# An S5 layer beside a SwiGLU: which DMA ring carries the first loads, and in which order the first products run

## The chip, the cores and the metric

The kernel runs on one core of one Trainium2 chip. The metric is the time of one execution on the device in microseconds (us), the median over runs. A profile is one further execution, taken by the hardware profiler, with its own time.

A core has five engines with their own instruction queues: TensorE (PE, matrix products; its weight loads are listed as PEld), VectorE (DVE), ScalarE (ACT), GpSimd (POOL) and SyncE (SP). Transfers between device memory and on-chip memory (DMAs) are issued here from two queues, SP's and ScalarE's. In the profile, q1 is the ring of transfers that SP issued, q10 the ring of those that ScalarE issued; both are worked off by the same sixteen transfer engines.

## What is computed

With x of shape (1, 2048, 512) in bfloat16, cut to what matters:

```python
xn = layernorm(x)                                   # over the 512 columns, no scale, eps 1e-5
# A: a diagonal state space layer with P = 512 complex states
dt = exp(log_dt); Lam = Lambda_re + 1j * Lambda_im
Lam_bar = exp(dt * Lam); B_bar = ((Lam_bar - 1) / Lam)[:, None] * (B_re + 1j * B_im)
Bu = xn @ B_bar.T
h[t] = Lam_bar * h[t - 1] + Bu[t]                   # over 2048 rows
yA = 2 * real(h @ C.T) + xn * Dskip
# B: a SwiGLU with F = 1792
yB = (silu(xn @ w1) * (xn @ w3)) @ w2
out = x + yA + yB
```

w1 and w3 are 512x1792, w2 is 1792x512.

## The kernel before

The 2048 rows are handled in four blocks of 512 (`x_blk[0..3]`), each block as four chunks of 128 rows. The columns D = 512 are four contraction tiles of 128 (`NDT = 4`, with the halves `lo` = tiles 0 and 1 and `hi` = tiles 2 and 3, `H = 2`). The hidden width F is fourteen tiles f of 128.

For each block: statistics and normalisation on DVE (`stats`, `aggr`, `normed`) with the reciprocal root on ScalarE for block 0 (`rstd_act`), a transpose into `xnT`, the gate and up products `g_ps` and `u_ps` on TensorE (`glu_mm`, L372) and their activations on ScalarE (`glu_up`), the state space input products `bu_ps` (L411), rotation and scan on DVE, and last the output products `y_ps` (L488, L493), the residual sum (L498) and the store (L499). The order of the work is written out by hand (`manual_schedule`): each engine runs its instructions in the order in which the program issues them, and small DVE tasks are taken from a queue by given costs.

The change lies in the first ten microseconds, the way to the first products of block 0:

- *Loads.* `load_rows` (L77) brings chunks of block 0: chunks 0 and 1 singly and chunks 2 and 3 together (256 KB). `load_w13` (L95) brings columns of w1 and w3; for the first four f tiles in two pieces each, by contraction half (`w1` low, `w1` high, `w3` low, `w3` high, 256 KB each, 1 KB per partition and contraction tile). `load_prm` (L109) brings one of three parameter vectors (`A_Lambda_re`, `A_Lambda_im`, `A_log_dt`, 1 KB each) into rows of `prm`, which TensorE later transposes (L544).
- *Queues.* SP issues rows 0, rows 1, w1 low, w1 high, w3 low, w3 high, then the next four f tiles of w1 and w3, block 1's rows, and so on. ScalarE issues Lambda_re, rows 2 and 3 together, Lambda_im, log_dt. Eight completion semaphores are used in turn for the DMAs, so that a DMA's issue waits for the landing of the one that had its semaphore before. The first column pieces of tiles 4 to 7 (w1) wait in this way for w1 low, w3 high for rows 1, log_dt for rows 0.
- *Transposes.* `turn` (L251) turns a chunk on TensorE into PSUM and `put` (L256 on ScalarE, L258 on DVE) copies it to `xnT`. Chunks 0 and 1 are turned and copied in halves; chunk 1's halves go through the two PSUM buffers of f = 2 (`t1`, views of `begun[2]`), so the products of f = 2 can't start before chunk 1 has been copied out.
- *First products.* `ahead` runs the products of f = 0, 1, 2 (`B3`) over the chunks that are there. `keep_warm` (L150) runs products of constants ahead of them, whose result isn't used.

Before, TensorE ran both halves of chunk 0's and chunk 1's transposes first, then, for f = 0, 1, 2, all low halves (chunk 0, then chunk 1, each 128 columns), then the high halves over both chunks at once (256 columns), then w3:

```python
    ahead((w1_sb,), B3, 0, 1, lo)
    ahead((w1_sb,), B3, 1, 1, lo, True)
    ahead((w1_sb,), B3, 0, 2, hi)
```

The last argument (`joins`) keeps a product from opening its accumulation anew, since chunk 0's sums in the same buffer are still open.

Of the kernel before, what the change touches and what calls it, by code (L numbers as in the profile page):

```python
# [20 lines left out]
def kernel(  # L21
# [24 lines left out]
    nc = tc.nc  # L46
# [6 lines left out]
    CPB = TBLK // P  # L53
    NSB = TBLK // SB
    NDT = D // P
# [20 lines left out]
    def load_rows(c0, c1, eng):  # L76
        eng.dma_start(out=x_blk[0][:, c0:c1, :], in_=xv[:, 0, c0:c1, :])  # L77
# [4 lines left out]
    w1_sb = const.tile([P, NDT, F], BF16, name="w1_sb")  # L82
    w3_sb = const.tile([P, NDT, F], BF16, name="w3_sb")
    w2_sb = const.tile([P, NFT, D], BF16, name="w2_sb")
    w1v = B_w1.rearrange("(t p) f -> p t f", p=P)
    w3v = B_w3.rearrange("(t p) f -> p t f", p=P)

    H = NDT // 2

    def load_w13(f0, f1, parts=1):  # L90
        fs = slice(f0 * P, f1 * P)
        for w_sb, wv in ((w1_sb, w1v), (w3_sb, w3v)):
            for i in range(parts):
                ds = slice(i * NDT // parts, (i + 1) * NDT // parts)
                nc.sync.dma_start(out=w_sb[:, ds, fs], in_=wv[:, ds, fs])  # L95

    dskip_row = const.tile([P, D], BF16, name="dskip_row")
    bt = [const.tile([P, NDT, PS], BF16, name=f"bt{ri}") for ri in range(2)]
# [9 lines left out]
    def load_prm(i, src, eng):  # L108
        eng.dma_start(out=prm[i * NPT:(i + 1) * NPT, :], in_=src.rearrange("(t p) -> t p", p=P))  # L109

    load_prm(0, A_Lambda_re, nc.scalar)
    load_rows(2, CPB, nc.scalar)
    load_prm(1, A_Lambda_im, nc.scalar)
    load_prm(2, A_log_dt, nc.scalar)
    load_w13(0, 4, 2)
    load_w13(4, 8)
    nc.sync.dma_start(out=x_blk[1], in_=xv[:, 1, :, :])
    load_w13(8, NFT)
    nc.sync.dma_start(out=dskip_row, in_=A_Dskip.partition_broadcast(P))
    load_turned(bt[0], A_B_re)  # L120
# [26 lines left out]
    def keep_warm(n, width=512):  # L147
        one = nc.const_aps.tensor_like(1.0, like=ident[:, 0:1])
        for _ in range(n):
            nc.tensor.matmul(out=begun[0][0][:, :width], lhsT=one.to_broadcast([P, P]), rhs=one.to_broadcast([P, width]),  # L150
                             start=True, stop=True)
# [10 lines left out]
    def stats(c):  # L162
        sums[c] = work.tile([P, 6], FP32, name="stats", bufs=4)
        nc.vector.bn_stats(out=sums[c], in_=x_blk[c // CPB][:, c % CPB, :])  # L164
# [4 lines left out]
    def rstd_act(c0, c1):  # L169
        y = rstd_all[:, c0:c1]  # L170
        nc.scalar.activation(out=y, in_=mv_all[:, c0:c1, 1], func=ACT.Ln, bias=LN_EPS)
        nc.scalar.activation(out=y, in_=y, func=ACT.Exp, scale=-0.5)
# [15 lines left out]
    def normed(c, parts=1):  # L188
        xn = work.tile([P, D], BF16, name="xn", bufs=8)
        for i in range(parts):  # L190
            ds = slice(i * D // parts, (i + 1) * D // parts)
            nc.vector.tensor_scalar(out=xn[:, ds], in0=x_blk[c // CPB][:, c % CPB, ds], scalar1=mv_all[:, c, 0:1],
                                    scalar2=rstd_all[:, c:c + 1], op0=ALU.subtract, op1=ALU.mult)
        return xn
# [54 lines left out]
    def turn(c, pxt, d0=0, d1=NDT):  # L249
        for dt in range(d0, d1):  # L250
            nc.tensor.transpose(out=pxt[:, dt - d0, :], in_=xn0[c][:, dt * P:(dt + 1) * P], identity=ident)  # L251

    def put(c, pxt, eng, d0=0, d1=NDT):
        dst = xnTs[0][:, d0:d1, c * P:(c + 1) * P]
        if eng is nc.scalar:
            nc.scalar.activation(out=dst, in_=pxt, func=ACT.Copy)  # L256
        else:
            nc.vector.tensor_copy(out=dst, in_=pxt)  # L258
# [110 lines left out]
    def glu_mm(b, f, w_sb, ps, ts, dts=range(NDT), joins=False):  # L369

        for dt in dts:
            nc.tensor.matmul(out=ps[:, ts], lhsT=w_sb[:, dt, f * P:(f + 1) * P], rhs=xnTs[b][:, dt, ts],  # L372
                             start=(dt == 0 and not joins), stop=(dt == NDT - 1))
# [128 lines left out]
    def ahead(w_sbs, fs, c, n=1, dts=range(NDT), joins=False):  # L502
        for f in fs:
            for w_sb in w_sbs:
                glu_mm(0, f, w_sb, begun[f][w_sb is w3_sb], slice(c * P, (c + n) * P), dts, joins)
# [13 lines left out]
    xn0[1] = normed(1, 2)  # L519
    turn(0, tb, H, NDT)  # L520
    put(0, tb, nc.scalar, H, NDT)
    keep_warm(2, P)
    turn(1, t1[0], 0, H)
    put(1, t1[0], nc.scalar, 0, H)
    turn(1, t1[1], H, NDT)
    put(1, t1[1], nc.scalar, H, NDT)
    stats(2)
    aggr(2)
    rstd_act(2, 3)
    stats(3)  # L530
    B3 = (0, 1, 2)
    lo, hi = range(H), range(H, NDT)
    ahead((w1_sb,), B3, 0, 1, lo)
    ahead((w1_sb,), B3, 1, 1, lo, True)
    ahead((w1_sb,), B3, 0, 2, hi)
    xn0[2] = normed(2)
    aggr(3)
    rstd_act(3, 4)
    ahead((w3_sb,), B3, 0, 2, lo)
    turn(2, t2)  # L540
    put(2, t2, nc.vector)
    xn0[3] = normed(3)
    ahead((w3_sb,), B3, 0, 2, hi)
    nc.tensor.transpose(out=pprm, in_=prm, identity=ident)  # L544
# [63 lines left out]
```

## Time and profile before

| | |
|---|---|
| median of 3 runs | 211.63 us (211.57 to 211.89) |
| the profiled execution's own time | 212.11 us |
| its span, first to last instruction | 210.3 us |
| PE busy | 206.6 us (98%), 1036 instructions |
| DVE busy | 173.5 us (82%) |
| ACT busy | 93.4 us (44%) |
| granted TensorE clock | 1.000 |
| moved by DMA | 13.69 MB, mean 65 GB/s |

A line of a group or of the timeline names the source line, the engine, the operation, out<-in by the program's names (w1, w3 and w2 are all `w_sb`), and the form. Matmuls are pipelined: the duration of one reaches from its start to its result, and the spacing of starts tells the rate. Queue lines (SPq, ACTq) are the issue of a DMA and not its transfer. An idle time in square brackets names what ended it.

### The profile page before, as it was taken

Reading aid. Unit: us, or ns where it says so; the run is one execution under the profiler, and the core shown is the slowest. Engines: PE = TensorE matmul, PEld = TensorE weight load, DVE = VectorE, ACT = ScalarE, POOL = GpSimd, SP = SyncE. Lnnn points to the kernel's source line nnn. Section 1 sums busy time; section 2 is a strip of 40 time slices with the busy share of each in tenths; the row PEclk is TensorE's granted clock in tenths of the full one; section 3 lists DMA queues with packets and bytes.
Section 4 is the critical chain, followed back from the end, with each engine's and each line's share of the span. In section 5 each row is a group of like instructions: output and inputs, shape, how many; then the busy total and the mean of one; then the engine's idle time right before and its main releaser. Section 6 shows DMA issues by size and latency. Waiting matters only on the chain.

```text
span 210.3 us, 2878 instructions
## 1 busy us (share of the span) xinstructions
PE 206.6 (98%) x1036; PEld 97.7 (46%) x1036; DVE 173.5 (82%) x346; ACT 93.4 (44%) x167; POOL 6.0 (3%) x27
## 2 busy tenths in 40 slices
PE   8999999999999999999999999999999999999994
PEld 3864444444444444444444444444444444444453
DVE  4699989989999999999999999999999999121111
ACT  3599967666666200066666600036666620000000
POOL 2010320000000000000000000000000000000000
PEclk9999999999999999999999999999999999999999
DMA  5999599944000000000004200100000000000110
GB/s 165 294 366 219 109 178 325 217 106 100 0 3 0 0 25 25 28 26 0 0 0 77 28 1 24 50 25 5 0 0 0 0 3 25 27 25 25 34 44 25
DMA packets 25014, 13.69 MB, mean 65 GB/s; under 512 B 15912, under 2 KB 25000, under 8 KB 25000
## 3 DMA queue, kind: packets, MB, share of 16 engines
q1 hardware_dynamic: 24704, 13.24, 26.1%
q10 hardware_dynamic: 296, 0.27, 0.4%
q8 instruction: 8, 0.13, 0.3%
q14 instruction: 6, 0.05, 0.1%
HBM read 7.74 MB, written 2.10 MB: 47 GB/s over the span
## 4 chain that ended last, share of the span: by engine, by line
PE 96%; DMA 2%; SPq 0%; DVE 0%; issue 0%
PE g_ps L372 23%; PE u_ps L372 23%; PE y_ps L488 23%; PE y_ps L493 13%; PE bu_ps L411 13%; DMA w_sb<-in_B_w_dram 2%; SPq L77 0%; PE xt_ps L251 0%; DVE o L498 0%; PE xt_ps L544 0%
## 5 line engine op out<-in xcount | busy, mean ns | idle before, releaser
L372 PEld LDWEIGHTS <-w_sb 128*128 128x128 bf16 x502 | 46.4, 98 | 50.6 <-DMA w_sb<-in_B_w_dram 0.6
L372 PE MATMUL g_ps<-xnT,w_sb 128*128 128x512 bf16 (+2 forms) x254 | 58.2, 354 | 0.3 <-DMA w_sb<-in_B_w_dram 0.3
L372 PE MATMUL u_ps<-xnT,w_sb 128*128 128x512 bf16 (+2 forms) x248 | 58.4, 358 | 0.0
L488 PE MATMUL y_ps<-w_sb,hgT 128*128 128x512 bf16 (+2 forms) x238 | 51.2, 366 | 0.0
L390 ACT ACTIVATE up<-u_ps 128x512 bf16<-128x512 f32 x56 | 34.0, 607 | 14.9 <-PE u_ps L372 14.9
L413 ACT ACTIVATE u<-bu_ps 128x512 bf16<-128x512 f32 x32 | 19.1, 597 | 46.3 <-PE bu_ps L411 46.3
L388 ACT ACTIVATE sl<-g_ps 128x512 bf16<-128x512 f32 x56 | 34.0, 608 | 9.9 <-PE g_ps L372 9.2
L445 DVE TENSOR_TENSOR_SCAN ab<-r_col,h,ab 128x256 bf16<-128x256 f32 x56 | 37.7, 733 | 0.2
L488 PEld LDWEIGHTS <-hgT 128*128 128x128 bf16 x238 | 22.8, 98 | 25.9
L498 DVE TENSOR_TENSOR o<-y_ps,x_blk 128x512 bf16<-128x512 f32 (+2 forms) x17 | 11.1, 654 | 24.3 <-PE y_ps L493 24.3
L493 PE MATMUL y_ps<-ct,h 128*128 128x512 bf16 (+2 forms) x136 | 30.4, 366 | 0.0
L411 PE MATMUL bu_ps<-xnT,bt 128*128 128x512 bf16 x128 | 28.1, 379 | 0.0
L397 DVE TENSOR_TENSOR hgT<-sl,up 128x512 bf16<-128x512 bf16 x56 | 22.9, 414 | 2.1 <-ACT up L390 2.1
L493 PEld LDWEIGHTS <-h 128*128 128x128 bf16 x136 | 13.0, 98 | 14.7
L411 PEld LDWEIGHTS <-bt 128*128 128x128 bf16 x128 | 12.5, 98 | 15.1
L164 DVE BATCH_NORM_STATS2 stats<-x_blk 128x6 f32<-128x512 bf16 x16 | 10.6, 675 | 2.5 <-DMA x_blk<-in_A_x_dram 2.5
L454 DVE TENSOR_TENSOR ab<-ab,tab_s 128x2048 bf16<-128x2048 bf16 x8 | 9.8, 1222 | 0.2
L450 DVE TENSOR_TENSOR ab<-ab,tab_c 128x2048 bf16<-128x2048 bf16 x8 | 9.8, 1222 | 0.1
L427 DVE TENSOR_TENSOR ab<-u,tab_x 128x2048 bf16<-128x2048 bf16 x8 | 9.7, 1219 | 0.0
L430 DVE TENSOR_TENSOR ab<-u,tab_y 128x2048 bf16<-128x2048 bf16 x8 | 9.7, 1218 | 0.0
L201 DVE TENSOR_TENSOR x_blk<-xd,x_blk 128x512 bf16<-128x512 bf16 x16 | 6.8, 426 | 0.5
L200 DVE TENSOR_TENSOR xd<-xn,dskip_row 128x512 bf16<-128x512 bf16 x16 | 6.7, 418 | 0.0
(76 smaller groups left out, 81.3 us busy)
## 6 DMA issues: line engine op xcount, KB each, us to landing
out_dram<-o SPq DMA_DIRECT2D x15, 128.0 KB, 1.7
w_sb<-in_B_w_dram SPq DMA_DIRECT2D x1, 1792.0 KB, 9.3
x_blk<-in_A_x_dram SPq DMA_DIRECT2D x3, 512.0 KB, 6.3
w_sb<-in_B_w_dram SPq DMA_DIRECT2D x2, 768.0 KB, 7.8
w_sb<-in_B_w_dram SPq DMA_DIRECT2D x4, 256.0 KB, 5.0
w_sb<-in_B_w_dram SPq DMA_DIRECT2D x2, 512.0 KB, 4.1
x_blk<-in_A_x_dram SPq DMA_DIRECT2D x2, 128.0 KB, 2.2
x_blk<-in_A_x_dram ACTq DMA_DIRECT2D x1, 256.0 KB, 4.7
```

The lines of the kernel that those rows point to most:

```text
L164: nc.vector.bn_stats(out=sums[c], in_=x_blk[c // CPB][:, c % CPB, :])
L372: nc.tensor.matmul(out=ps[:, ts], lhsT=w_sb[:, dt, f * P:(f + 1) * P], rhs=xnTs[b][:, dt, ts], start=(dt == 0 and not joins), stop=(dt == ...
L388: nc.scalar.activation(out=sl16, in_=g_ps, func=ACT.Silu)
L390: nc.scalar.activation(out=up16, in_=u_ps, func=ACT.Copy)
L397: nc.vector.tensor_tensor(out=hg[b][:, f, :], in0=sl16, in1=up16, op=ALU.mult)
L411: nc.tensor.matmul(out=u_ps, lhsT=bt[ri][:, dt, pt * P:(pt + 1) * P], rhs=xnTs[b][:, dt, :], start=(dt == 0), stop=(dt == NDT - 1))
L413: nc.scalar.activation(out=u16[:, :, pt, ri, :], in_=u_ps.rearrange("p (s t) -> p s t", s=NSB), func=ACT.Copy)
L445: nc.vector.tensor_tensor_scan(out=a[:, pt, 2 * ri + 1, :], data0=r_b, data1=a[:, pt, 2 * ri, :], initial=init, op0=ALU.mult, op1=ALU.add)
L450: nc.vector.tensor_tensor(out=a[:, :, 0::2, :], in0=a[:, :, 1::2, :], in1=tab_b("c"), op=ALU.mult)
L488: nc.tensor.matmul(out=y_ps[:, ds], lhsT=hg[b][:, f, cl * P:(cl + 1) * P], rhs=w2_sb[:, f, ds], start=(f == 0), stop=False)
L493: nc.tensor.matmul(out=y_ps[:, ds], lhsT=h_tiles[i][:, pt, ri, h_ts], rhs=ct[ri][:, pt, ds], start=False, stop=(pt == NPT - 1 and ri == 1))
L498: nc.vector.tensor_tensor(out=o16[:, ds], in0=y_ps[:, ds], in1=x_blk[b][:, cl, ds], op=ALU.add)
```

## The change

Rows 2 and 3, Lambda_im and log_dt move from ScalarE's queue to SP's, and w1 low and w1 high from SP's to ScalarE's. ScalarE issues Lambda_re, w1 low, w1 high. SP issues rows 0, rows 1, rows 2 and 3, Lambda_im, log_dt, w3 low, w3 high, and from there on the same as before. With the other order the semaphores fall differently: the w1 piece of tiles 4 to 7 waits for the landing of rows 2 and 3, w3 low for that of rows 0.

On TensorE the first products of w1 run in another order: chunk 0's low half for f = 0 and 1 stands between the two halves of chunk 1's transposes; then, for f = 0 and 1, chunk 0 high, chunk 1 low, chunk 1 high; then f = 2 over both chunks and all four contraction tiles. The work from w3's products on is in the same order as before.

```diff
-    def load_w13(f0, f1, parts=1):
+    def load_w(w_sb, wv, f0, f1, eng, ds=slice(0, NDT)):
         fs = slice(f0 * P, f1 * P)
-        for w_sb, wv in ((w1_sb, w1v), (w3_sb, w3v)):
-            for i in range(parts):
-                ds = slice(i * NDT // parts, (i + 1) * NDT // parts)
-                nc.sync.dma_start(out=w_sb[:, ds, fs], in_=wv[:, ds, fs])
+        eng.dma_start(out=w_sb[:, ds, fs], in_=wv[:, ds, fs])
+
+    def load_w13(f0, f1):
+        load_w(w1_sb, w1v, f0, f1, nc.sync)
+        load_w(w3_sb, w3v, f0, f1, nc.sync)
...
+    low, high = slice(0, H), slice(H, NDT)
     load_prm(0, A_Lambda_re, nc.scalar)
-    load_rows(2, CPB, nc.scalar)
-    load_prm(1, A_Lambda_im, nc.scalar)
-    load_prm(2, A_log_dt, nc.scalar)
-    load_w13(0, 4, 2)
+    load_w(w1_sb, w1v, 0, 4, nc.scalar, low)
+    load_w(w1_sb, w1v, 0, 4, nc.scalar, high)
+    load_rows(2, CPB, nc.sync)
+    load_prm(1, A_Lambda_im, nc.sync)
+    load_prm(2, A_log_dt, nc.sync)
+    load_w(w3_sb, w3v, 0, 4, nc.sync, low)
+    load_w(w3_sb, w3v, 0, 4, nc.sync, high)
     load_w13(4, 8)
...
     put(0, tb, nc.scalar, H, NDT)
+    B3 = (0, 1, 2)
+    lo, hi = range(H), range(H, NDT)
     keep_warm(2, P)
     turn(1, t1[0], 0, H)
     put(1, t1[0], nc.scalar, 0, H)
+    ahead((w1_sb,), (0, 1), 0, 1, lo)
     turn(1, t1[1], H, NDT)
     put(1, t1[1], nc.scalar, H, NDT)
     stats(2)
     aggr(2)
     rstd_act(2, 3)
     stats(3)
-    B3 = (0, 1, 2)
-    lo, hi = range(H), range(H, NDT)
-    ahead((w1_sb,), B3, 0, 1, lo)
-    ahead((w1_sb,), B3, 1, 1, lo, True)
-    ahead((w1_sb,), B3, 0, 2, hi)
+    ahead((w1_sb,), (0, 1), 0, 1, hi)
+    ahead((w1_sb,), (0, 1), 1, 1, lo)
+    ahead((w1_sb,), (0, 1), 1, 1, hi)
+    ahead((w1_sb,), (2,), 0, 2)
```

## Prediction, made before the changed kernel was run

> **What bounds the kernel now.** I read the page first: its chain of waits says which engine sets the end.
>
> ```profile
> PE 96%; DMA 2%; SPq 0%; DVE 0%; issue 0%
> PE g_ps L372 23%; PE u_ps L372 23%; PE y_ps L488 23%; PE y_ps L493 13%; PE bu_ps L411 13%; DMA w_sb<-in_B_w_dram 2%; SPq L77 0%; PE xt_ps L251 0%; DVE o L498 0%; PE xt_ps L544 0%
> ```
>
> TensorE carries 96%, and ahead of it stands one load, of w1 or w3 (2%, 4.8 us). The timeline of PE where that load ends is next (start, duration, line, operation, count, idle before it):
>
> ```profile
> 5.54 0.42 PE L251 MATMUL g_ps<-ident,xn 128*128 128x128 bf16 x2
> 5.76 0.41 PE L251 MATMUL u_ps<-ident,xn 128*128 128x128 bf16 x2
> 6.48 1.51 PE L372 MATMUL g_ps<-xnT,w_sb 128*128 128x128 bf16 x18 [0.31 <-DMA w_sb<-in_B_w_dram]
> 7.83 0.83 PE L372 MATMUL u_ps<-xnT,w_sb 128*128 128x256 bf16 x6
> ```
>
> The reader is to see one wait of 0.31 us ahead of the first product at 6.48, and none behind it. The busy time in windows, asked from there to PE's last instruction, shows how long that lasts (stretch, its length, then busy time by engine):
>
> ```profile
> 6.48:207.66 201.18, 201.18 (x1013) 95.21 (x1013) 170.11 (x334) 90.19 (x159) 4.64 (x19) 1.00 0.26 61
> ```
>
> PE is busy for all of 201.18 us. So any delay of the first products reaches the end one to one (no later idle time absorbs it), and nothing that the change does later than these products can help. The tail behind 207.66 (DVE, last store) stays.
>
> Third, the loads that feed the first products. Issues, from the timeline of all engines:
>
> ```profile
> 0.72 0.87 SPq L77 DMA_DIRECT2D x_blk<-in_A_x_dram  x2
> 0.94 0.55 ACTq L109 DMA_DIRECT2D prm<-in_A_Lambda_re_dram  x1
> 1.53 0.44 ACTq L77 DMA_DIRECT2D x_blk<-in_A_x_dram  x1
> 1.64 5.73 SPq L95 DMA_DIRECT2D w_sb<-in_B_w_dram  x6
> ```
>
> SP's six are w1 low half (1.64), w1 high (2.11), w3 low (2.62), w3 high (3.40), then the next 512 columns of each (6.45, 6.86). By the trace's semaphore events rows 2–3 land at 6.24, w1 low at 6.43, w1 high 7.11, w3 low 7.78, w3 high 8.44. The first products use them at 6.48, 7.16, 7.83 and 8.72: each of the first three lands about 0.05 us ahead of its user. The last fact needed is how the two rings share the transfer engines. The DMA queues of the window 4.0 to 4.5 us, when rows 2–3 (q10, ScalarE's ring) and w1 low (q1, SP's) both move (packets, MB, share of 16 engines):
>
> ```profile
> q10 hardware_dynamic: 85, 0.09, 48.4%
> q1 hardware_dynamic: 80, 0.08, 47.7%
> ```
>
> An even split. And on one ring alone a 256 KB piece takes 0.67 us (6.43, 7.11, 7.78, 8.44).
>
> **The change part by part.**
>
> *Which ring.* Rows 2–3 and w1 low change places. They are the same size (256 KB in pieces of 1 KB), issued within 0.11 us of each other, so I let them swap landings: w1 low at 6.24, 0.19 us earlier. The bounds are 5.47, where fifteen of its sixteen completion counts for rows 2–3 stood before (one transfer engine runs 0.76 us behind the rest in all five pieces), and 6.43 (no gain).
>
> *w1 high* is issued on ScalarE at about 2.0 instead of 2.11, which is worth nothing, because data and not issue is late. Before, it followed w1 low on a ring that was alone by then, and w3 low waited behind it. Now w3 low heads the other ring (issued at about 2.9: behind rows 2–3, two parameter loads of 0.27 to 0.55 us each on the issuing queue, and the landing of rows 0, whose semaphore it reuses, at 2.87), so the two share. On the late engine: at 6.24 w1 low is done, and rows 2–3 have the 0.19 us left that separated the two before. Shared, that takes 0.38: rows 2–3 land at 6.62, and w1 high has 0.19 of its 0.67 us. The other 0.48 is shared with w3 low: 0.96. w1 high lands at 6.62 + 0.96 = 7.58 instead of 7.11; w3 low still at 7.78, since the sum of bytes is unchanged. The bounds are 6.91 (ScalarE's ring served alone from 6.24 on) and 7.78 (as late as w3 low). I take 7.58, since the even split is what the rows show.
>
> The Trainium skill speaks against expecting more from a second ring (DMA: Bandwidth & Descriptors, "Issuing engines are not separate DMA queues"): DMAs from any engine end up on the same sixteen transfer engines and interleave, and several issuers save issue time only. The even split above agrees, and the sum by that rule is the same.
>
> *Order of the first products.* On PE the first 24 units (one unit is 128 columns, 0.056 us apart in the trace; 256 columns take 0.109) stay 24: before 12x128 and 6x256, now 16x128 and 4x256. Two more instructions cost nothing, because spacing goes by columns. What moves is what can run while w1 high is missing. Before: all twelve low products, 0.67 us, which covered the 6.48 to 7.16 gap between the pieces. Now: four (f = 0 and 1, rows 0), 0.22 us, and the two transposes of row block 1's high half, which stood in the idle time at 5.76 and now stand behind the wait on w1 low, 0.11 us. Everything else on PE queues behind the first high product. Row by row: restart 6.24 + 0.05 = 6.29; four products to 6.51; two transposes to 6.62; wait for w1 high to 7.58 + 0.05 = 7.63; then 12x0.056 + 4x0.109 = 1.11, to 8.74. Before, w3's first product started at 7.83. So **+0.91 us**.
>
> *Who waits behind the moved transposes.* ScalarE's copy of that half (L256) moves from 6.28 to about 6.9, ends at 7.3, and its next user on PE runs at about 8.1; ScalarE's rstd for row 2 follows at about 7.4. Free here; without the wait for w1 high it would cost (third rival).
>
> *Rows 2–3 later* (6.62 instead of 6.24): DVE's statistics (L164) start at 6.64 instead of 6.27, the normalised row 2 ends at 8.46 instead of 8.09. PE transposes it at 8.49 + 0.91 = 9.40. Free, with 0.9 us to spare. *Parameters on SP* (lam_im and log_dt): read by the transpose at 9.27 (L544), landing near 7. Free by over 2 us. *The next w1 piece* (columns 512 to 1023) waited for w1 low's landing and now waits for rows 2–3's: issue 6.64 instead of 6.45, landing 10.57 + 0.19, first use 12.33 + 0.91. Free; w3's behind it likewise. w3 low is needed at 8.74, w3 high at 9.63; both have landed.
>
> **Sum.** +0.91 us on the profiled execution: span 210.3 to 211.2, own time 212.11 to 213.02. The median of the runs is 211.63, 0.48 below that execution; on it, **212.5 us**.
>
> **The rivals.**
>
> 1. *Rings alternate in whole shares.* If a transfer engine drains w1 high's sixteen pieces before it turns to w3 low, w1 high lands at 7.11 as before, PE restarts at 7.16 and reaches w3 at 8.27: +0.44, 212.07. Against: from 5.13 to 5.73 us the late engine's last eight data packets on q10 start 85 ns apart, by the trace's packet records, and a packet takes 46 ns, so single packets alternate. The Trainium skill gives the rule in the same page ("Queues, rings and completion order"): an engine round-robins between rows and takes some 9 to 17 descriptors from one before it switches. The 85 ns spacing disagrees with it in this case. Chance 0.12.
> 2. *The late engine is on time.* With the landings of the other fifteen, w3 low is in at 7.08 and w1 high 0.2 before that, 6.89; restart 6.94, w3 at 8.05: +0.22, 211.85. It lags in every piece of the one trace that I have, but not in rows 0 and 1, so its cause is open. Chance 0.12.
> 3. *Faster: ScalarE's ring leads.* If w1's two pieces run ahead of SP's rows, both terms turn. Breakeven is w1 high landing before 6.67 (7.83 − 1.11 − 0.05) and w1 low before 6.12, because the way from it through the moved transposes and their copy is also serial: four products 0.22, transposes 0.11, 0.24 to the copy, 0.38 copy, 0.05, then 0.22 and 0.44 of products, 1.71 with the start. At best PE starts low products at 5.76, where spacing is still 0.107 per unit: 5.76 + 0.43 + 0.21, copy to about 7.03, then 0.66 to 7.71. That gains 0.12 us (0.3 if the clock were up by then): 211.3 to 211.5. For it: w1's issue is now ahead of the rows' by 0.11. Against: the even split. Chance 0.12, of which 0.04 for a gain over 0.2%.
> 4. *The clock.* PE's unit takes 0.107 up to 5.86 and 0.056 from 6.55 on. A pause of 0.62 us between starts did no harm; one of about 1.0 us in this place isn't shown. If the rate fell back or came up late, twenty units would cost 1.07 us more: +2.0, 213.6. Chance 0.06.
>
> **How the numbers follow.** Forecast: w1 high shared with w3 low, +0.55 to +1.15 (w1 high between 7.2 and 7.8), chance 0.58. The range takes in the first two rivals and 0.15 for the spread of runs above the top: 211.75 to 212.95; it leaves out most of rivals 3 and 4, 0.18. The bound of 0.2% is 0.42 us, about what a measurement of this kernel can tell from no change. Slower by more: the forecast, the clock, and 0.07 of rival 1, which sits on the bound: 0.71. Within: rival 2, the rest of 1, and 0.08 of 3: 0.25. Faster: 0.04.
>
> **What would show it.** In the profile after: four 128-column products at about 6.3, two transposes, then a second PE wait of about 1.0 us released by a load of w_sb; w3's first product near 8.74; statistics of row 2 near 6.6; no other PE idle time. It is wrong if w1 high lands by 7.1 (sharing isn't even), or if w3's first product starts before 7.83.

## The result, and the profile after

The changed kernel takes 212.12 us (median of 16 runs, 211.85 to 212.57), the kernel before 211.75 (16 runs beside it, 211.57 to 212.14): ratio **1.0021**, 95% interval 1.0014 to 1.0027, or 0.37 us between the medians. The profiled execution after took 212.06 us with a span of 210.2, against 212.11 and 210.3 before. The two profiles alone thus show no loss; why is the first thing to explain.

The chain of waits after has the same shape:

```profile
PE 96%; DMA 2%; ACT 0%; ACTq 0%; DVE 0%; issue 0%
```

The issues, from the timeline of all engines (start, duration, queue, line):

```profile
0.72 1.34 SPq L77 DMA_DIRECT2D x_blk<-in_A_x_dram  x3
1.55 0.96 ACTq L92 DMA_DIRECT2D w_sb<-in_B_w_dram  x2
2.11 0.41 SPq L110 DMA_DIRECT2D prm<-in_A_Lambda_im_dram  x1
2.57 0.25 SPq L110 DMA_DIRECT2D prm<-in_A_log_dt_dram  x1
2.87 0.91 SPq L92 DMA_DIRECT2D w_sb<-in_B_w_dram  x2
```

w1 low is issued at 1.55 and w1 high at 2.03 on ScalarE, w3 low at 2.87 on SP, as worked out. PE's timeline after:

```profile
5.53 0.28 PE L256 MATMUL g_ps<-ident,xn 128*128 128x128 bf16 x2
5.75 0.40 PE L377 MATMUL g_ps<-xnT,w_sb 128*128 128x128 bf16 x4
5.98 0.28 PE L256 MATMUL u_ps<-ident,xn 128*128 128x128 bf16 x2
6.65 1.28 PE L377 MATMUL g_ps<-xnT,w_sb 128*128 128x128 bf16 x16 [0.39 <-DMA w_sb<-in_B_w_dram]
7.77 0.71 PE L377 MATMUL u_ps<-xnT,w_sb 128*128 128x256 bf16 x5
```

The reader is to see the order of the prediction: four products, two transposes, then a wait for a load (0.39 us) in front of twenty units. w3's first product (`u_ps`) starts at 7.77. From 6.65 on PE is busy without a pause, as it was before (the busy time in windows):

```profile
6.65:207.59 200.94, 200.94 (x1011) 95.09 (x1011) 169.59 (x333) 90.04 (x159) 4.63 (x19) 1.00 0.24 61
```

So one number says it all: the **start of w3's first product**. In thirteen of the fourteen profiled executions of this study, of ten different kernels, an execution's own time minus this start is 204.25 to 204.29 us (212.11 − 7.83 = 204.28 before, 212.06 − 7.77 = 204.29 after); the fourteenth is that of e11, below. Nothing behind that start differs by more than 0.04 us. The table has what sets it, with landings by the semaphore events of the traces:

| profile | w1 low | w1 high | w3 low | w3's first product | behind |
|---|---|---|---|---|---|
| before, first | 6.43 | 7.11 | 7.78 | 7.83 | w3 low + 0.05 |
| before, again (e0) | 5.85 | 6.59 | 7.31 | 7.36 | w3 low + 0.05 |
| after | 5.70 | 6.60 | 7.33 | 7.77 | w1 high + 1.16 |

Before, w3's first product starts 0.05 us behind the landing of its own weights; TensorE was done with w1 by then, but only just: twelve units behind w1 high end at 7.11 + 0.05 + 0.67 = 7.83 in the first profile and at 7.31 in e0, so there was next to no room for more of them. After, it starts 1.16 us behind w1 high (0.05 + twenty units, 1.11), and w3 low has been there for 0.44 us. w3 low lands 0.73 us behind w1 high, so 1.16 − 0.05 − 0.73 = 0.38 us are lost, close to the 0.37 by which the medians differ. The first profile of before hid this, since its loads landed late.

### The profile page after: what moved, and what is told of

The parts are those of the page before. It is cut to its first block, busy times and chain, and to the rows that moved or that the text cites. A ratio compares the mean times of both kernels' runs of the same rounds, so it can differ in the third digit from the quotient of the medians.

```text
span 210.2 us, 2882 instructions
## 1 busy us (share of the span) xinstructions
PE 206.4 (98%) x1038; PEld 97.7 (46%) x1038; DVE 173.4 (82%) x346; ACT 93.4 (44%) x167; POOL 6.0 (3%) x27
## 4 chain that ended last, share of the span: by engine, by line
PE 96%; DMA 2%; ACT 0%; ACTq 0%; DVE 0%; issue 0%
PE u_ps L377 23%; PE y_ps L493 23%; PE g_ps L377 23%; PE y_ps L498 13%; PE bu_ps L416 13%; DMA w_sb<-in_B_w_dram 2%; ACT L81 0%; ACTq L92 0%; PE xt_ps L256 0%; DVE o L503 0%; PE xt_ps L551 0%
## 5 line engine op out<-in xcount | busy, mean ns | idle before, releaser
L377 PE MATMUL g_ps<-xnT,w_sb 128*128 128x512 bf16 (+1 forms) x256 | 58.4, 352 | 0.4 <-DMA w_sb<-in_B_w_dram 0.4
```

## The experiments

Two theories stood against each other from the start. *Order*: the twenty units queued behind w1 high are the loss. *Sharing*: w1 high itself lands later, because w3 low moves beside it (the prediction had both, 0.44 and 0.47). A third view had to be cleared first: the 0.76 us by which one transfer engine lagged in the first profile.

The edits of e1, e3, e4, e5 and e11 are shown against the changed kernel.

**e0: the kernel before, once more.** No edit.

> The kernel before, once more. Theory A (a chance delay): in the first profile of before one of the sixteen transfer engines ran 0.76 us behind in all first pieces, and that was this one execution; here w1's first piece lands near 5.7 us instead of 6.43 and its second near 6.35, TensorE starts w1's products near 6.0 and w3's first product near 7.35 instead of 7.83, span 209.8 to 209.9, time near 211.6. Theory B (the delay belongs to this ring layout): w1's first piece at 6.4 again, w3's first product at 7.83, span 210.3.

Measured 211.63 us, span 209.9. The lag is gone: w1 low at 5.85, w3 low at 7.31. PE's timeline:

```profile
5.71 0.28 PE L251 MATMUL u_ps<-ident,xn 128*128 128x128 bf16 x2
5.90 1.58 PE L372 MATMUL g_ps<-xnT,w_sb 128*128 128x128 bf16 x18
7.36 0.83 PE L372 MATMUL u_ps<-xnT,w_sb 128*128 128x256 bf16 x6
```

No wait stands in brackets; 7.36 is 0.47 earlier than in the first profile, and the time 0.48 less. The first profile was one draw at the late end of this kernel's 211.57 to 212.14. But w1 high lands at 6.59, later than the 6.35 expected here: the pieces scatter.

**e1: the new order alone**, on the old rings.

```diff
-    load_w(w1_sb, w1v, 0, 4, nc.scalar, low)
-    load_w(w1_sb, w1v, 0, 4, nc.scalar, high)
-    load_rows(2, CPB, nc.sync)
...
+    load_rows(2, CPB, nc.scalar)
...
+    load_w(w1_sb, w1v, 0, 4, nc.sync, low)
+    load_w(w1_sb, w1v, 0, 4, nc.sync, high)
```

> Loads on the rings of before, TensorE's first products in the new order. Theory A with sharing (w1's second piece is late because w3's first piece shares the transfer engines with it): on the old rings that piece lands near 6.35, so the new order waits for it from 6.1 to 6.4 and reaches w3 at 7.5, 0.15 us behind before: ratio 1.0005 to 1.001. Rival (the order alone costs all of it): ratio 1.002, w3's first product near 7.77. Rival (the rings alone cost it): ratio 1.000.

Ratio 1.0028 (1.0017 to 1.0039): more than expected under sharing, and as much as the whole change. In its profile w1 high lands at 6.83, w3 low at 7.52, and w3's first product starts at 8.00, again 1.16 behind w1 high:

```profile
6.88 1.28 PE L377 MATMUL g_ps<-xnT,w_sb 128*128 128x128 bf16 x16
8.00 0.38 PE L377 MATMUL u_ps<-xnT,w_sb 128*128 128x256 bf16 x2
```

The order alone costs all of it. The number missed because I had taken w1 high at 6.35 on the old ring.

**e2: the new rings alone**, in the old order (`ahead` as before the change).

> Loads on the new rings, TensorE's first products in the order of before. Theory A with sharing: w1's second piece lands near 6.6 as in the changed kernel, but twelve low products (0.67 us from 6.0 on) stand ahead of the first product that needs it, so the wait is hidden: w3's first product near 7.35, ratio 1.000 (0.9995 to 1.0005). Rival (the rings alone cost it): ratio 1.002. Under either, rows 2 and 3 land near 5.9.

Ratio 1.0002 (0.9993 to 1.0010). PE's timeline:

```profile
5.98 1.61 PE L377 MATMUL g_ps<-xnT,w_sb 128*128 128x128 bf16 x18
7.50 0.83 PE L377 MATMUL u_ps<-xnT,w_sb 128*128 128x256 bf16 x6
```

w3 low landed at 7.45: the start is 0.05 behind it, as before. The rings alone cost nothing that the interval shows.

**e5: a dose between the two orders.** Sixteen units behind w1 high instead of twenty (or twelve, before).

```diff
-    ahead((w1_sb,), (0, 1), 0, 1, hi)
-    ahead((w1_sb,), (0, 1), 1, 1, lo)
-    ahead((w1_sb,), (0, 1), 1, 1, hi)
+    ahead((w1_sb,), (0, 1), 1, 1, lo, True)
+    ahead((w1_sb,), (0, 1), 0, 2, hi)
```

> The changed kernel with row chunk 1's low products of f = 0 and 1 ahead of the first high product: 16 units of 128 columns stand behind the wait for w1's second piece instead of 20 (before: 12). Theory order: the time follows the units behind that wait, w3's first product starts 0.94 us behind the piece's landing instead of 1.16, which is -0.22 us: ratio to before 1.0010. Rival (the wait itself, not what is queued behind it, sets the loss): ratio 1.002.

Ratio 1.0011 (1.0003 to 1.0020), the expected value. w1 high landed at 6.56 and w3's first product started at 7.50: 0.94 behind, as worked out for sixteen units:

```profile
6.22 1.45 PE L377 MATMUL g_ps<-xnT,w_sb 128*128 128x128 bf16 x12
7.50 0.82 PE L377 MATMUL u_ps<-xnT,w_sb 128*128 128x256 bf16 x6
```

The twelve are four low products of 128 columns and eight of 256 columns, the sixteen units. The loss follows what is queued behind the wait.

**e3: w3 held back**, with all that SP issues behind it, to take sharing away.

```diff
+    def load_late():
+        nc.gpsimd.tensor_copy(out=w3_sb[:, 0, 0:1], in_=mv_all[:, 1, 0:1])
+        load_w(w3_sb, w3v, 0, 4, nc.sync, low)
...
     aggr(1)
+    load_late()
```

> The changed kernel, but w3's two first pieces are held back on SP until row chunk 1's statistics are done (a one-column copy by GpSimd into w3's first column, which the load then overwrites, makes SP wait), issue near 4.9 instead of 2.87 us. Theory sharing: w1's second piece now has the engines to itself behind rows 2 and 3 and lands near 6.3 instead of 6.6; w1's products are done near 7.45 instead of 7.77; w3's first piece lands between 7.0 and 7.9, so the end moves by -0.3 to +0.1 us against the changed kernel. Rival (w1's second piece is late for its own issue or its place on ScalarE's ring, not for sharing): it lands at 6.6 again, and the time is that of the changed kernel or more.

Ratio 1.0020 (1.0011 to 1.0029), no gain on the changed kernel: the medians are 212.16 and 212.12. In the profile w3 low was issued at 4.96, and w1 high landed at 6.89, 0.89 us behind w1 low (6.00), against 0.90 in the changed kernel. e2 and e5, which issue the same loads as the changed kernel, have 0.78 and 1.04. So taking w3 low away brought w1 high no nearer to w1 low. This is one execution, in which one of the sixteen completion counts of w1 high came 0.40 us behind the other fifteen (at 6.49), so that a share of 0.1 or 0.2 us isn't excluded. The time adds little: held back, w3 low landed at 7.70, and its product couldn't have started before 7.75 in any case. In this profile too the product follows 1.16 behind (8.05).

**e4: the parameters behind w3**, so that w3 low follows rows 2 and 3 directly (issue at 2.10 instead of 2.87).

```diff
-    load_prm(1, A_Lambda_im, nc.sync)
-    load_prm(2, A_log_dt, nc.sync)
     load_w(w3_sb, w3v, 0, 4, nc.sync, low)
     load_w(w3_sb, w3v, 0, 4, nc.sync, high)
+    load_prm(1, A_Lambda_im, nc.sync)
+    load_prm(2, A_log_dt, nc.sync)
```

> The changed kernel with Lambda_im and log_dt behind w3's two pieces on SP instead of ahead of them. Theory gap (w1's second piece did not have to share because SP's ring stood nearly empty between rows 2 and 3 and w3's first piece, for the two small loads): the empty stretch of the q1 ring between 5.0 and 5.75 us is filled, w3's first piece shares, w1's second piece lands 0.15 to 0.4 us after the 6.60 of the changed kernel, ratio to before 1.003 to 1.004. Rival (rows 2 and 3 alone hold w3 back, the small loads do nothing): landings and time as in the changed kernel, ratio 1.002.

Here sharing appears. The DMA queues from 5.0 to 5.75 us, ring, packets, MB, share of sixteen engines, first of the changed kernel:

```profile
q10 hardware_dynamic: 221, 0.21, 80.7%
q1 hardware_dynamic: 84, 0.07, 28.7%
```

and then of e4:

```profile
q10 hardware_dynamic: 160, 0.16, 64.0%
q1 hardware_dynamic: 111, 0.11, 42.7%
```

In the changed kernel ScalarE's ring (w1 high) takes three quarters of the bytes in this stretch, because SP's has run nearly dry behind rows 2 and 3; in e4 w3 low fills it. w1 high landed at 7.09, 1.77 us behind w1 low (5.31), against 0.90 in the changed kernel, and PE waited:

```profile
7.13 1.28 PE L377 MATMUL g_ps<-xnT,w_sb 128*128 128x128 bf16 x16 [1.11 <-ACT rstd_all L177]
```

The bracket names ScalarE's `rstd` for row chunk 2, which ended at 7.12; these products don't read it. The wait ended 0.05 us behind the landing of w1 high, as in the changed kernel. This is the wait of about 1.0 us that the prediction had for the changed kernel. Seven of the eleven executions took 212.39 to 212.73 (212.54 in the middle, 1.0039 of 211.72, as expected); the other four 214.46 to 214.72, with a mean granted clock of 0.991 to 0.992 where the seven have 1.000. They make the overall ratio 1.0073 (1.0045 to 1.0102), which the expectation didn't have. What e4 doesn't separate: whether the two small loads kept w3 low back in the changed kernel, or the issue that waited for rows 0's landing.

**e9 and e10: e4 again**, for a profile of a long execution.

> The kernel with the parameters behind w3 once more, for its profile: four of its eleven timed executions took about 2.1 us longer than the other seven. Theory clock: in such an execution the wait of about 1.1 us ahead of w1's second half lets TensorE's rate fall, so that products start 0.107 us apart per 128 columns for some microseconds behind it (212.5 if it doesn't happen here, 214.5 if it does). Rival (another cause, a load that lands late): spacing stays at 0.056 and one wait is 2 us longer.

> The same kernel and the same two theories, one more draw: 212.5 with a spacing of 0.056 us behind the wait, or 214.5 with 0.107 (clock) or with one longer wait (a late load).

Neither draw was a long one: 212.66 and 212.85, waits of 1.23 and 0.93 us, spacing 0.056 behind them. Both add to the table's rule: w3's first product 1.16 behind w1 high (7.24 to 8.41, 7.43 to 8.59).

**e11: w1 high behind both of w3's pieces on SP, the parameters behind that**, to make the wait longer.

```diff
-    load_w(w1_sb, w1v, 0, 4, nc.scalar, high)
     load_rows(2, CPB, nc.sync)
+    load_w(w3_sb, w3v, 0, 4, nc.sync, low)
+    load_w(w3_sb, w3v, 0, 4, nc.sync, high)
+    load_w(w1_sb, w1v, 0, 4, nc.sync, high)
     load_prm(1, A_Lambda_im, nc.sync)
     load_prm(2, A_log_dt, nc.sync)
-    load_w(w3_sb, w3v, 0, 4, nc.sync, low)
-    load_w(w3_sb, w3v, 0, 4, nc.sync, high)
```

> The changed kernel with w1's second piece behind both of w3's on SP, the parameters behind that: it lands near 8.0, w1's products wait about 2 us for it and are done 1.16 us later, w3's product starts near 9.2, +1.4 us against the changed kernel (213.5), if only the landing counts. Theory clock: a wait of 2 us lowers TensorE's rate in more executions than the wait of 1.1 us did (four of eleven), then products start 0.107 us apart per 128 columns behind it and the execution takes 2 us more, 215.5. Rival: spacing 0.056 in the profile and all executions within 0.5 us of 213.5.

Six executions of 213.53 to 215.81, median 215.06 (ratio 1.0142, 1.0109 to 1.0175); four of the six with a granted clock of 0.991 to 0.992. The other two, 213.53 and 213.73, are at what was expected if only the landing counts. The profile fell on one of the four (214.99); w1 high landed at 8.20 in it. PE's timeline and the windows:

```profile
8.24 2.31 PE L377 MATMUL g_ps<-xnT,w_sb 128*128 128x128 bf16 x16 [1.70 <-DMA w_sb<-in_B_w_dram]
10.35 1.17 PE L377 MATMUL u_ps<-xnT,w_sb 128*128 128x256 bf16 x6
```

```profile
6.40:8.24 1.84, 0.14 (x3) 0.00 (x1) 1.71 (x5) 0.97 (x5) 0.00 (x0) 0.84 0.72 190
8.24:11.13 2.89, 2.89 (x20) 2.45 (x21) 0.00 (x0) 0.34 (x2) 0.00 (x0) 0.51 1.06 367
11.13:12.23 1.10, 1.10 (x14) 1.00 (x12) 0.45 (x2) 0.00 (x0) 0.00 (x0) 1.00 1.10 349
```

The column behind the last bracketed count is the granted clock: it falls during the wait, stays at 0.51 for 2.89 us of products (0.107 us per unit) and comes back. Asked in finer windows, it is 1.00 up to 7.64 and 0.50 from there to 11.05, 3.41 us in all. At the full rate the 28 units of the second window (twenty of w1, eight of w3) would have taken 1.56 us, so 1.33 are lost. Part of that lies behind the start of w3's first product, which is why this profile alone has 204.64 for own time minus that start.

**e6, e7 and e8: smaller first pieces**, three f tiles (192 KB) instead of four, since only three are used by the first products; on the kernel before, on the changed one, and on e2.

```diff
-    load_w13(0, 4, 2)
-    load_w13(4, 8)
+    load_w13(0, 3, 2)
+    load_w13(3, 8)
```

> The kernel before with first pieces of three f tiles (192 KB) instead of four (256 KB), which are the three that the first products use; the next pieces take the fourth. Theory landings: before is bound by the landing of w3's first piece (in its two profiles its first user started 0.05 us behind it); four pieces, of which three count, shrink by a quarter, so that piece lands 0.4 to 0.5 us earlier and TensorE's own work sets the start, near 7.25 to 7.35: 211.55 to 211.65, ratio 0.9990 to 0.9995. Rival (before is bound by TensorE's work already): ratio 1.000.

> The changed kernel with first pieces of three f tiles. Theory landings: w1's second piece lands 0.3 us earlier (two of the pieces ahead of it or in it are a quarter smaller), w3's first product starts 1.16 us behind that, near 7.45: -0.3 us against the changed kernel, ratio to before 1.0005 to 1.001. Rival (the start of the pieces and not their size sets the landing): ratio 1.002.

> The new rings, TensorE's order of before, first pieces of three f tiles. Theory landings and order: w1's second piece lands near 6.2 and w3's first near 6.8, both ahead of their users in this order, so TensorE's own work from its first product (near 5.9) sets the start of w3's products, near 7.3: 211.55 to 211.65, ratio to before 0.999 to 0.9997. Rival (nothing is left to gain, landings of w1's first piece and the copies to xnT set it): ratio 1.000.

e7 gives back the loss: 1.0002 (0.9994 to 1.0011), more than expected. w1 high lands at 6.18, w3's first product starts at 7.34, 1.16 behind:

```profile
6.23 1.28 PE L377 MATMUL g_ps<-xnT,w_sb 128*128 128x128 bf16 x16
7.34 0.82 PE L377 MATMUL u_ps<-xnT,w_sb 128*128 128x256 bf16 x6
```

That is the first theory from its other side: with the order unchanged, an earlier w1 high is worth its whole advance. e6 is at 0.9996 (0.9988 to 1.0005) and e8 at 1.0000 (0.9991 to 1.0009), so no version beats the kernel before by more than the interval, and the gain expected of these two isn't there. In their profiles w3 low has been there for 0.47 us (e6) and 0.38 us (e8) when its first product starts, so its load doesn't set the start; TensorE's own work from its first product on does, with the copies to `xnT` that it needs. In e6 that is 24 units behind a w1 low that landed late, at 6.23 (start at 7.61, 1.38 behind it).

## Why the prediction was right or wrong

- **The number: inside the range, but not for the forecast's reason.** +0.9 us was forecast and 0.37 came. The range, 211.75 to 212.95, holds 212.12 because it had been widened to take in the first two rivals; the forecast's own span, +0.55 to +1.15, doesn't hold it. Whether the loss is more or less than 0.2% the runs don't tell: 1.0021 sits on that bound. That the number fits is in part luck.
- **Its own signs of being wrong: both came.** w1 high landed at 6.60, ahead of 7.1, and w3's first product started at 7.77, ahead of 7.83. Both marks were taken from the execution with late loads, so they tell less than they seem to: against e0's 7.36 the product did come later. w1 high came as it did in e0 (6.59), where the even split would have put it 0.47 us later.
- **Direction and bound: right.** PE without a pause behind its first products, every delay passed on to the end. Thirteen of the fourteen profiles hold to it within 0.04 us, and the fourteenth departs from it by a falling clock.
- **The order term, +0.44 us: right.** It is the difference between twelve and twenty units behind w1 high, 0.67 and 1.11, of which the 0.05 us of room in e0 come off. The medians differ by 0.37, and e1, e2 and e5 put the loss on the order, in proportion to the units.
- **The sharing term, +0.47: wrong, and this is the step that failed.** "Now w3 low heads the other ring (...), so the two share." It did not head it in time: SP's ring was still moving rows 2 and 3 and then ran nearly dry, so w1 high had most of the engines to itself, and followed w1 low after 0.90 us instead of the predicted 1.34. Without w3 low, the prediction's own sum gives 6.62 + 0.48 = 7.10, 0.86 behind w1 low; the changed kernel, e2 and e5 lie around that, with 0.90, 0.78 and 1.04. The wait was 0.39 us instead of about 1.0. The even split of two full rings, read in the window 4.0 to 4.5, was a true reading, but what the second ring would hold a microsecond later was an assumption. e4, where w3 low does follow at once, has the predicted wait.
- **The gain of 0.19 us on w1 low:** the changed kernel's lands at 5.70, against 5.85 in e0 and 6.43 in the first profile; single draws, from which the size can't be told.
- **The base of the sum: a late draw.** Every landing in the sum came from one execution with a lagging engine. The second rival said so ("it lags in every piece of the one trace that I have"), and e0 showed it. The text set the median 0.48 us below that execution, without asking which of its waits the median didn't have.
- **Free terms: right.** Row chunk 2's transposes at 8.42 found their data; the parameters, the next w1 piece and ScalarE's moved copy cost nothing.
- **First rival** (w1 high drained ahead, +0.44, 212.07): its time is nearest to the measured 212.12, but by coincidence. Its mechanism isn't what the runs show: the ring of w3 low ran nearly dry (28.7% in the stretch shown) and was not passed over; where w3 low was there, in e4, w1 high did have to share.
- **Third rival** (faster): w1 high would have had to land before w3 low by over 1.11 us; it was 0.73.
- **Fourth rival** (the clock): not in this kernel, where the wait is 0.39 us and every execution has a mean clock of 0.999 or 1.000. Where a wait is longer it is real, and its price was too low: the prediction put 1.07 us on a clock that falls (its +2.0 has the wait of 0.91 in it), and e4's four long executions are 2.0 us above the other seven. None of the four was profiled; that it is the clock rests on their mean of 0.991 to 0.992. One stretch of 3.41 us at half rate, as in e11, would give about that (an estimate: half of 3.41, over 213 us, is 0.8%). It would explain at most 1.7 of the 2.0 us; the rest stays open.

## What to carry to other kernels

When an in-order engine waits for a load, the price of the wait is what is queued behind it minus the time until the next load that it would have waited for anyway: put all work that doesn't need the load ahead of it. Take landings from more than one execution before costing a step with them, and ask of a second ring not only how it shares but what it will hold at that time.

## What the runs showed of the hardware that was not expected

- TensorE's rate fell after a short wait. In e11 it was idle for 1.70 us, and the granted clock was already 0.53 in the window 7.60 to 8.24, about 1.1 us into the wait; 2.89 us of products then ran at half rate. The Trainium skill (TensorE: Matmul & The Clock Gate, "Why this matters for your kernels") warns of idle gaps above about 3 us between bursts of products. The measurement decides: here a shorter one was enough. How short is not shown. In e9 a wait of 1.23 us left the clock at 1.000; e11 had another idle time of 0.56 us shortly before, ahead of its transposes at 5.19, and whether that counts is not shown. In e4 four of eleven executions have the lower mean clock, and what their waits were isn't known. The 0.39 us wait of the changed kernel did no harm.
- The same load lands at different times in executions of the same order of issues: w1 high at 7.11, 6.59 and 6.83 in the three profiles with the old rings and full pieces. What makes one transfer engine lag stays open.
